# Linear attention and a token-mixing MLP on one core: nine casting DMAs of GpSimd issued in one row, and the second batch's k^T v in two halves

## The chip, the cores and the metric

The kernel runs on one core of a Trainium2 chip. The metric is the device time of one execution in microseconds (us). The engines are named as in the profile: PE (TensorE, matmuls; PEld its weight loads), DVE (VectorE), ACT (ScalarE), POOL (GpSimd) and SP (SyncE, which here only issues DMAs).

## The reference

```python
kv  = einsum('bhsd,bhse->bhde', k, v)          # k^T v per head
out = einsum('bhsd,bhde->bhse', q, kv)         # q.kv
out = out / sqrt(mean(out*out, -1) + 1e-6) * g_norm
x   = out with the heads side by side          # 8 batches, 576 tokens, 512 channels
u   = x + lam * (w_tok @ (alpha1 * x + beta1)) # mixing over tokens
y   = u + lam * (relu((alpha2 * u + beta2) @ w_ch1) @ w_ch2)
```

There are 8 batches, 8 heads, 576 tokens and a head size of 64; w_ch1 is 512 x 2048, w_ch2 2048 x 512. Inputs and output are float32.

## The kernel before, in words

**A planner orders everything.** `Prog.op` records each operation with its engine (or engines to choose from), a cost in us, what it reads and writes, and a priority. `schedule` plays the operations through a list scheduler: whenever an engine is free it takes the first ready operation of its queue in order of priority, and it also picks the PSUM banks. For DMAs it carries a model of the transfer: those of SP follow each other, those of POOL start some time after their issue (the line with `free[e] + 0.3`) and take their share from those of SP. The result is a fixed order for each engine, and `synchronize` adds the semaphore waits. An operation with `at=` has a fixed priority, and `after=` adds dependences that no data needs; `slack` lets the planner take an operation for ready that long after its inputs. A changed cost or gate can therefore move instructions on all engines; at run time each engine runs its list in order.

**The start.** The loads of q, k and v for the first batch come in two halves of the heads (L519, on SP). For each half PE makes k^T v (L616), transposes q (L584, L577) and makes q.kv (L706, L711). ACT squares (L743), DVE sums (L745), ACT and DVE make the reciprocal root (L748, L751), and DVE writes the normalized rows xm and their tail xtl (L767). Then `rt = xm * e_bc` (L771) and `xm = xm * g` (L774), here on POOL. `e_bc`, the product of alpha1, lam and g on all partitions, is made by PE (L1058) behind the second half's k^T v and copied by ACT (L506). Mixing over tokens is `tok_half`: L833 on PE with rt, then an addition by DVE (L845); PE transposes the result (L866), and the first layer of the MLP begins with L966 and goes on with L935. Until that first L966, PE fills its idle time with dummy matmuls on zeros (L1345) that the planner puts in.

**POOL's casting DMAs.** Weights in bfloat16 come by DMAs that cast, all issued by POOL: `w_tok` in four pieces and a rest (`wst`, L1112, and `wst4`, L1115), and `w_ch1` in four quarters (`w1`, L1267). Each has a priority and a gate in `after`, the load that must have landed before POOL may issue it:

```python
tgate = [("qf", 0), ("kf", 1)]                            # w_tok 0,1 / 2,3
gate = [("vf", 1), ("vf", 1), ("wst", 3), ("wst", 3)]     # w1 quarters 0 to 3
```

PE transposes w_tok with an identity matrix (L1159, L1180) and makes sums over its rows (L1202). The bias of the first layer, beta2 times w_ch1, is made by PE for each quarter (L1228) from b2hl, two small rows that POOL writes (L1071, L1073). SP loads the second batch's q, k and v only when the second quarter of w1 has landed. w_ch2 is loaded in float32 by SP (stg, L1274) and multiplied by lam on DVE or POOL (L1279).

**Further on.** The second batch's k^T v is one group of 144 small matmuls between groups of the first batch's first layer, its result copied by ACT and DVE in four copies (kvr, L506, L507). Then follow the second batch's q.kv, the second layer (L1000), mixing over tokens for the second batch (L799, L812), its transposes (L905), and the same stages for each later batch (first layer L950 for odd batches, L935 for even ones).

Of the kernel before, what the change touches and what calls it, by code (L numbers as in the profile page):

```python
# [54 lines left out]
class Prog:  # L55
# [79 lines left out]
    def schedule(self):  # L135
# [6 lines left out]
        free = {e: 0.0 for e in queues}  # L142
# [77 lines left out]
        while left:  # L220
            progressed = False
            for e, q in queues.items():
                while q and free[e] <= t + 1e-9:
# [64 lines left out]
                    if pick.lat is not None:  # L288
                        if e == "SP":
                            dma_free = max(dma_free, t + (2.5 if t < 3 else 1.25)) + pick.lat  # L290
                            pick.end = dma_free + 1.3
                            moving.append(pick)
                        elif e == "POOL":
                            s = max(free[e] + 0.3, pool_dma)
                            left_ = max(0.0, dma_free - s)
                            pool_dma = s + pick.lat + min(left_, pick.lat)
                            for y in moving:
                                if y.end - 1.3 > s:
                                    y.end += min(pick.lat, y.end - 1.3 - s)
                                    events.add(y.end)  # L300
                            dma_free = max(dma_free, s) + pick.lat
                            pick.end = pool_dma + 1.6
                        else:
                            pick.end = t + pick.lat + 3.0
                    else:
                        pick.end = free[e] + (0.35 if e == "PE" else 0.15)
# [110 lines left out]
def bass_transnormer_attn__then__resmlp_affine_kernel(  # L417
# [15 lines left out]
    with ExitStack() as stack:  # L433
        P = Prog(nc, stack)

        def sb(name, shape, dt):
            return stack.enter_context(nc.sbuf_tensor(name, shape, dt))
# [17 lines left out]
        kf = sb("kf", [128, 4, 9, DH], F32)  # L455
        vf = sb("vf", [128, 4, 9, DH], F32)
        qf = sb("qf", [128, 4, 9, DH], F32)
# [16 lines left out]
        wst4 = sb("wst4", [64, S], BF16)  # L474
        smask = sb("smask", [128, 128], BF16)
        w1 = sb("w1", [128, 4, FF], BF16)
# [7 lines left out]
        wst = ht[:].rearrange("p j t -> p (j t)")[:, 0:2304].rearrange("p (c s) -> p c s", c=4)  # L484
# [7 lines left out]
        def act_us(n):  # L492
            return 0.19 + n / 1200.0
# [15 lines left out]
        HALVES = (slice(0, 4), slice(4, 8))  # L509
# [4 lines left out]
        def halves(hs):  # L514
            return range(hs.start // 4, hs.stop // 4)
# [87 lines left out]
        def kv_groups(b, parts=ALL):  # L603
            def group(hs):
                t = P.ptile(2)
                h0, np_ = hs.start, (hs.stop - hs.start) // 4
                aa = halves(hs)

                def f(e):
                    for x_ in range(np_):  # L610
                        for c in range(9):
                            for i in range(2):
                                for y in range(2):
                                    x = h0 // 2 + 2 * x_ + i
                                    rows = slice(64 * y, 64 * y + 64)
                                    m = e.matmul(  # L616
                                        t.ap(slice(64 * i, 64 * i + 64))[
                                            :, y, 64 * x_:64 * x_ + 64],
                                        kf[rows, x, c], vf[rows, x, c], start=(c == 0),
                                        stop=(c == 8), tile_position=(64 * y, 64 * i))  # L620
                    return m
                P.op("PE", 0.2 + 1.06 * np_, f, cold=True, w=[t, ("kvp", hs.start)],
                     r=[("kf", a) for a in aa] + [("vf", a) for a in aa])

                def src(z):
                    return t.ap(slice(64 * z, 64 * z + 64))[:, :, 0:64 * np_].rearrange(
                        "p y (x d) -> p x y d", d=64)

                def heads(ap, z):
                    return ap[:, :, 2 * z:2 * z + 2]  # L630
                if b < R32:
                    prev = {}
                    for k_, (z, r_) in enumerate(((0, 0), (1, 0), (1, 1), (0, 1))):
                        o = heads(kvr[64 * r_:64 * r_ + 64, hs, 64 * r_:64 * r_ + 64].rearrange(
                            "p (x h) d -> p x h d", h=4), z)
                        prev[z] = [P.op(
                            "ACT" if k_ % 2 == 0 else "DVE",
                            act_us(128 * np_) if k_ % 2 == 0 else dve_us(128 * np_),
                            lambda e, o=o, z=z: copy(e, o, src(z)), hold=[t],
                            r=[("kvp", hs.start), "kvz"], w=[("kvr", a, z, r_) for a in aa],  # L640
                            after=prev.get(z, []))]
                    return
                kv5 = kvd[:].rearrange("p (x h) i d -> p x h i d", h=4)
                for z in range(2):
                    for r_ in range(2):
                        hi = heads(kv5[64 * r_:64 * r_ + 64], z)[:, :, :, 0]
                        P.op("ACT", act_us(256), lambda e, z=z, hi=hi: e.activation(  # L647
                            hi, src(z), ACT.Identity), r=[t], w=[("kvd", z, r_, 0)])
                for z in range(2):
                    for r_ in range(2):  # L650
                        hi, lo = (heads(kv5[64 * r_:64 * r_ + 64], z)[:, :, :, i]
                                  for i in range(2))
                        P.op("DVE", dve_us(256), lambda e, z=z, hi=hi, lo=lo: e.tensor_tensor(
                            out=lo, in0=src(z), in1=hi, op=ALU.subtract),
                            r=[t, ("kvd", z, r_, 0)], w=[("kvd", z, r_, 1)])
            for hs in parts:
                yield lambda hs=hs: group(hs)
# [447 lines left out]
        for i, hs in enumerate(HALVES):  # L1105
            for n in "kvq":
                load(n, 0, hs, sp["%s%d" % (n, i)])
        tgate = [("qf", 0), ("kf", 1)]
        wrows = moe_w_tok.rearrange("(u s c) t -> u s c t", s=32, c=9)
        for x in range(2):  # L1110
            for u in (2 * x, 2 * x + 1):
                P.op("POOL", 0.5, lambda e, u=u: e.dma_start(  # L1112
                    wst[:, u, :], wrows[u % 2, :, u // 2:u // 2 + 7:2]),
                    w=[("wst", u)], dma_us=0.85, at=-9003.0 + u, after=P.lastw[tgate[x]])
        P.op("POOL", 0.4, lambda e: e.dma_start(wst4[:], moe_w_tok[8:576:9, :]),  # L1115
             w=[("wst", 4)], dma_us=0.9, at=-8998.5, after=P.lastw[("wst", 3)])
        for n, dst, src in (("lam", lam_bc, moe_lam), ("a2", a2_bc[:], moe_alpha2),
                            ("g", g_bc[:], g_norm)):
            P.op("SP", 0.6, lambda e, dst=dst, src=src: e.dma_start(
# [1 line left out]
                 dma_us=0.8 if n != "g" else 0.3, at=sp[n])  # L1121
# [18 lines left out]
             w=["identb"])  # L1140
# [96 lines left out]
        def run(gens):  # L1237
            for gen in gens:
                for f in gen:
                    f()  # L1240
# [19 lines left out]
                    for i in range(2):  # L1260
                        P.readers.setdefault(("hth", j, i), []).append(o)

        gate = [("vf", 1), ("vf", 1), ("wst", 3), ("wst", 3)]

        def load_w(i):
            if i < 4:
                P.op("POOL", 0.9, lambda e: e.dma_start(  # L1267
                    w1[:, :, 512 * i:512 * i + 512], moe_w_ch1[
                        :, 512 * i:512 * i + 512].rearrange("(j p) f -> p j f", p=128)),
                    w=[("w1", i)], dma_us=2.6, at=-9000.0 + i, after=P.lastw[gate[i]])  # L1270
                bias_groups(i)
            else:
                n = i - 4
                P.op("SP", 0.6, lambda e: e.dma_start(  # L1274
                    stg[:, i % 3], moe_w_ch2[512 * n:512 * n + 512, :].rearrange(
                        "(j p) c -> p j c", p=128)), w=[("stg", i % 3)], dma_us=2.6,
                    at=sp["w%d" % i])
                for hh in range(4):
                    P.op(dve_pool(512), 0, lambda e, hh=hh: e.tensor_tensor(  # L1279
                        out=w2[:, 4 * n + hh, :], in0=stg[:, i % 3, hh], in1=lam_bc[:],  # L1280
                        op=ALU.mult), r=[("stg", i % 3), "lam"], w=[("w2p", n, hh)], pri=60,
                        after=u0, port=True)
                P.lastw[("w2", n)] = [y for hh in range(4) for y in P.lastw[("w2p", n, hh)]]
# [10 lines left out]
        load_kv(1, at=lambda n: sp["B" + n])  # L1294
        load_q(1, at=lambda n: sp["B" + n])
        u0 = P.lastw[("a2t", 0)] + P.lastw[("a2t", 2)]
        run([kv_groups(1), qt_groups(1)])
        for i in range(4, 8):
            load_w(i)
        for y in range(2):  # L1300
# [14 lines left out]
        for b in range(NB):  # L1315
# [17 lines left out]
            if more:  # L1333
                if b == 0:
                    P.op("POOL", 0.9, lambda e: e.memset(qtt[:], 0.0),
                         w=[("qt", 2, y) for y in range(2)])
# [45 lines left out]
```

## Time and profile before

| | |
|---|---|
| median of 9 runs | 366.28 us |
| lowest and highest run | 364.58 and 367.3 us |
| the profiled execution | 365.74 us, its span 363.7 us |
| PE busy | 351.6 us, 97% of the span |
| DVE, ACT, POOL busy | 211.0, 143.0, 115.8 us |
| DMA | 56.41 MB, mean 155 GB/s |
| granted clock, mean | 0.994 |

The span is the time from the first to the last instruction; the rest of the profiled execution's time lies around it. Busy PE is matmuls one after the other, also dummy ones. "Idle before" in a row is the idle time of the engine ahead of that instruction, with what ended it; "issue" means that the profile shows nothing that it waited for. The chain that ended last is followed back from the last instruction, at each step to what released it. The views of the chain, the timeline, the stretches and the DMA queues give times from the start of the span.

### The profile page before, as it was taken

The numbers are of one execution on the slowest core, as the hardware profiler recorded it, in microseconds if no ns is written. First come the engines' busy times: TensorE is split into PE (matmuls) and PEld (weight loads), VectorE is DVE, ScalarE is ACT, GpSimd is POOL, SyncE is SP. The second block draws the span as 40 slices with busy tenths as digits, with TensorE's granted clock in tenths as the row PEclk, the third lists the DMA queues.
The fourth block names the chain that finished last, engine by engine and source line by source line (L and its number), as shares of the span: only waits on it lengthen the run. The fifth ranks groups of instructions, "written<-read, shape, count | busy, mean of one in ns | idle before, by whom it ended". The sixth has DMA issues, their size and how long they took to land.

```text
span 363.7 us, 7875 instructions
## 1 busy us (share of the span) xinstructions
PE 351.6 (97%) x3504; PEld 210.8 (58%) x3296; DVE 211.0 (58%) x319; ACT 143.0 (39%) x253; POOL 115.8 (32%) x97
## 2 busy tenths in 40 slices
PE   8999799999999999999999999999999999999996
PEld 6977574366754554457654554457754554457644
DVE  3565779992577189733885189723884189620021
ACT  2763156327741156207730158007730156007600
POOL 3794177230065005800281015800661005400000
PEclk9999989999999999999999999999999999999999
DMA  7999994038775768557917694758945610331023
GB/s 285 214 213 349 383 383 183 0 45 110 206 285 111 120 162 329 101 111 128 370 32 113 123 309 154 102 113 140 357 62 106 140 31 0 74 87 31 0 59 87
DMA packets 67558, 56.41 MB, mean 155 GB/s; under 512 B 45552, under 2 KB 48452, under 8 KB 67524
## 3 DMA queue, kind: packets, MB, share of 16 engines
q1 hardware_dynamic: 64704, 53.14, 55.8%
q0 software_dynamic: 2768, 2.76, 4.8%
q8 instruction: 27, 0.44, 0.5%
q14 instruction: 7, 0.06, 0.0%
q10 hardware_dynamic: 52, 0.01, 0.0%
HBM read 38.60 MB, written 9.44 MB: 132 GB/s over the span
## 4 chain that ended last, share of the span: by engine, by line
PE 85%; DVE 6%; POOL 4%; issue 2%; DMA 2%; SPq 0%; ACT 0%; POOLq 0%; DVEq 0%
PE ps L1000 32%; PE ps L950 19%; PE ps L935 13%; PE ps L799 7%; PE ps L616 5%; PE ps L696 2%; PE ps L410 2%; DMA qf<-in_q_dram 2%; POOL rt L771 2%; POOL xm L774 1%; DVE rt L771 1%; PE ps L584 1%; PE ps L812 1%; DVE w L1279 1%; PE ps L966 1%
## 5 line engine op out<-in xcount | busy, mean ns | idle before, releaser
L1000 PE MATMUL ps<-w,ht 128*128 128x512 bf16 (+1 forms) x569 | 125.8, 373 | 1.8 <-issue 1.0
L1000 PEld LDWEIGHTS ps<-w,ht 128*128 128x128 bf16 x592 | 56.9, 98 | 64.0 <-issue 1.2
L924 ACT ACTIVATE ht<-ps,bias 128x640 bf16<-128x640 f32 (+2 forms) x100 | 73.5, 739 | 50.4 <-PE ps L950 37.9
L950 PE MATMUL ps<-a2t,w 128*128 128x320 bf16 x512 | 71.9, 299 | 0.0
L774 POOL TENSOR_TENSOR xm<-xm,g_bc 128x1024 f32<-128x1024 f32 (+1 forms) x18 | 36.2, 2012 | 109.7 <-DVE rt L771 109.2
L950 PEld LDWEIGHTS ps<-a2t,w 128*128 128x128 bf16 x512 | 49.4, 98 | 20.4 <-DVE xm L767 0.3
L935 PE MATMUL ps<-a2t,w 128*128 128x512 bf16 x231 | 54.0, 382 | 0.7 <-issue 0.2
L1011 DVE TENSOR_TENSOR xm<-ps,xm 128x512 f32<-128x512 f32 (+1 forms) x33 | 22.1, 672 | 52.4 <-PE ps L1000 52.4
L647 ACT ACTIVATE kvd<-ps 64x256 bf16<-64x256 f32 x24 | 9.1, 378 | 95.6 <-PE ps L616 95.4
L745 DVE TENSOR_REDUCE small<-sq 128x16 f32<-128x1024 f32 (+3 forms) x30 | 25.0, 846 | 23.0 <-ACT sq L743 22.8
L935 PEld LDWEIGHTS ps<-a2t,w 128*128 128x128 bf16 x240 | 22.7, 99 | 25.5 <-issue 0.6
L799 PE MATMUL ps<-rt,wt 128*128 128x512 bf16 x140 | 31.4, 379 | 0.4 <-DVE rt L771 0.4
L925 DVE TENSOR_SCALAR ht<-ps,bias 128x512 bf16<-128x512 f32 (+2 forms) x32 | 23.7, 745 | 11.7 <-PE ps L935 4.9
L548 POOL TENSOR_TENSOR qs<-qf,qs 128x512 bf16<-128x512 f32 x13 | 16.6, 1275 | 28.5 <-ACT qs L506 27.8
L743 ACT ACTIVATE sq<-ps 128x1024 f32<-128x1024 f32 (+3 forms) x30 | 21.7, 735 | 10.2 <-PE ps L410 8.2
L799 PEld LDWEIGHTS ps<-rt,wt 128*128 128x128 bf16 x140 | 13.6, 98 | 17.2 <-DVE rt L771 0.9
L783 DVE TENSOR_TENSOR xm<-ps,xm 128x512 f32<-128x512 f32 x28 | 19.0, 687 | 7.8 <-PE ps L799 7.5
L1011 DVE TENSOR_TENSOR xtl<-ps,xtl 128x512 f32<-128x512 f32 x4 | 2.8, 692 | 35.5 <-PE ps L1000 35.5
L785 POOL TENSOR_TENSOR a2b<-xm,a_bc 128x512 bf16<-128x512 f32 x12 | 17.4, 1450 | 14.9 <-DVE xm L783 9.5
L616 PE MATMUL ps<-vf,kf 64*64 64x64 f32 x1152 | 19.3, 220 | 3.0 <-issue 2.5
L616 PEld LDWEIGHTS ps<-vf,kf 64*64 64x64 f32 x1152 | 17.9, 135 | 6.1 <-issue 5.4
L767 DVE TENSOR_TENSOR xm<-ps,small 128x1024 f32<-128x1024 f32 (+1 forms) x20 | 20.1, 1004 | 0.3
(106 smaller groups left out, 331.6 us busy)
## 6 DMA issues: line engine op xcount, KB each, us to landing
kf<-in_k_dram SPq DMA_DIRECT2D x7, 1152.0 KB, 6.1
vf<-in_v_dram SPq DMA_DIRECT2D x7, 1152.0 KB, 9.8
qf<-in_q_dram SPq DMA_DIRECT2D x7, 1152.0 KB, 11.5
out_dram<-xm SPq DMA_DIRECT2D x62, 128.0 KB, 2.4
stg<-in_moe_w_ch_dram SPq DMA_DIRECT2D x4, 1024.0 KB, 16.6
w<-in_moe_w_ch_dram POOLq DMA_DIRECT2D x4, 512.0 KB, 8.6
kf<-in_k_dram SPq DMA_DIRECT2D x2, 576.0 KB, 6.0
vf<-in_v_dram SPq DMA_DIRECT2D x2, 576.0 KB, 7.1
```

What stands on the lines that cost most here:

```text
L616: m = e.matmul(t.ap(slice(64 * i, 64 * i + 64))[:, y, 64 * x_:64 * x_ + 64], kf[rows, x, c], vf[rows, x, c], start=(c == 0), stop=(c == 8) ...
L743: P.op("ACT", act_us(64 * m), lambda e: e.activation(both(sqv), raw(), ACT.Square), r=[t], w=[("sq", sqs)])
L745: P.op("DVE", dve_us(64 * m), lambda e: e.tensor_reduce(out=smv, in_=sqv, axis=AX.X, op=ALU.add), r=[("sq", sqs)], w=[("sm", sms)], pri=-20)
L767: P.op("DVE", dve_us(64 * m), lambda e: e.tensor_tensor(out=x3, in0=raw(), in1=inv(), op=ALU.mult), r=[t, ("sm", sms)], w=xk, pri=-200)
L774: P.op(dve_pool(64 * m) if b < 2 else "POOL", pool_us(64 * m), lambda e: e.tensor_tensor(out=x3, in0=x3, in1=gb, op=ALU.mult), r=xk + ["g" ...
L799: m = e.matmul(t.flat(), wt[:, sc if sc < 4 else 4 + b % 2, 128 * c:128 * c + 128], rt[:, rs(b, sc), :], start=(sc == 0), stop=(sc == 4))
L924: return e.activation(dst, src(), ACT.Relu, bias=bi)
L925: return e.tensor_scalar(out=dst, in0=src(), scalar1=bi, scalar2=0.0, op0=ALU.add, op1=ALU.max)
L935: m = e.matmul(t.flat(), w1[:, dj, 128 * fj:128 * fj + 128], a2t[:, dj, 0:512], start=(dj == 0), stop=(dj == 3))
L950: m = e.matmul(t.ap()[:, i, 0:320], w1[:, dj, 128 * fj:128 * fj + 128], a2t[:, dj, 320 * i:320 * i + 320], start=(dj == 0), stop=(dj == 3))
L1000: m = e.matmul(t.flat()[:, 0:m_], ht[:, fj, 128 * c:128 * c + 128], w2[:, fj, lo:hi], start=(fj == 0), stop=(fj == 15))
L1011: P.op("DVE", dve_us(m_), lambda e: e.tensor_tensor(out=x, in0=t.flat()[:, 0:m_], in1=x, op=ALU.add), r=[t] + keys, w=keys)
```

## The change

It does four things. All w_tok pieces and the first two quarters of w1 are now gated by the first half of q, and wst4 and the last two quarters by the second half of k; with the new priorities all nine casting DMAs stand in one row on POOL, ahead of the first product with e_bc. The planner's model has data of a POOL DMA start 1.2 instead of 0.3 us after the issue, the issue costs 0.6 or 0.8 us, and the loads of w1 get a slack of 1.0. And the second batch's k^T v is recorded in two halves of the heads (36 matmuls of the code each, every one of which shows as two in the profile).

```diff
-                            s = max(free[e] + 0.3, pool_dma)
+                            s = max(free[e] + 1.2, pool_dma)
...
-        tgate = [("qf", 0), ("kf", 1)]
+        tgate = [("qf", 0), ("qf", 0)]
...
-                P.op("POOL", 0.5, lambda e, u=u: e.dma_start(
+                P.op("POOL", 0.6, lambda e, u=u: e.dma_start(
                     wst[:, u, :], wrows[u % 2, :, u // 2:u // 2 + 7:2]),
                     w=[("wst", u)], dma_us=0.85, at=-9003.0 + u, after=P.lastw[tgate[x]])
-        P.op("POOL", 0.4, lambda e: e.dma_start(wst4[:], moe_w_tok[8:576:9, :]),
-             w=[("wst", 4)], dma_us=0.9, at=-8998.5, after=P.lastw[("wst", 3)])
+        P.op("POOL", 0.6, lambda e: e.dma_start(wst4[:], moe_w_tok[8:576:9, :]),
+             w=[("wst", 4)], dma_us=0.9, at=-8998.0, after=P.lastw[("kf", 1)])
...
-        gate = [("vf", 1), ("vf", 1), ("wst", 3), ("wst", 3)]
+        gate = [("qf", 0), ("qf", 0), ("kf", 1), ("kf", 1)]
...
-                P.op("POOL", 0.9, lambda e: e.dma_start(
+                P.op("POOL", 0.8, lambda e: e.dma_start(
                     w1[:, :, 512 * i:512 * i + 512], moe_w_ch1[
                         :, 512 * i:512 * i + 512].rearrange("(j p) f -> p j f", p=128)),
-                    w=[("w1", i)], dma_us=2.6, at=-9000.0 + i, after=P.lastw[gate[i]])
+                    w=[("w1", i)], dma_us=2.6, at=-8999.5 + i, after=P.lastw[gate[i]],
+                    slack=1.0)
...
-        run([kv_groups(1), qt_groups(1)])
+        run([kv_groups(1, HALVES), qt_groups(1)])
```

The built order of POOL in the changed kernel: four w_tok pieces, quarters 0 and 1, wst4, quarters 2 and 3, the cast of b2hl, two products rt, xm, rt's tail, xm, b2hl's difference, xtl, and then the second half (two rt, its tail, two xm). On PE the transposes of wst4 and their sums stand ahead of L966, and four L935 stand between the halves of the second batch's k^T v.

## The prediction

> **What bounds the kernel now.** I began with the page's second part, the 40 slices, each 9.1 us long.
>
> ```profile
> PE   8999799999999999999999999999999999999996
> ...
> PEclk9999989999999999999999999999999999999999
> DMA  7999994038775768557917694758945610331023
> ```
>
> TensorE (PE) is busy everywhere; the only dent after the first slice is the fifth, 36 to 45 us, and the only dip of its clock is in the slice behind it. DMA is full up to 55 us. So a change to the start pays only by what it takes off PE before about 75 us; from there the rows are PE without holes. Next I read the chain that ended last, in order of time, for the start.
>
> ```profile
> 15.43 1.28 POOL rt L771
> ...
> 18.06 0.29 issue
> 18.35 0.59 POOL wst L1115
> 18.94 0.31 POOL w L1267
> 19.25 0.45 issue
> 19.70 0.76 POOL w L1267
> 20.46 0.77 POOL rt L771
> ...
> 28.82 1.28 POOL xm L774
> ...
> 31.81 3.49 PE ps L966 x32
> ```
>
> From 15.43 to 30.10 GpSimd (POOL) is the chain. Ahead of that it waits 1.37 us for e_bc (its timeline says); it multiplies, and at 18.06 stops multiplying for 2.40 us to issue three casting DMAs. 1.71 us after its last product, at 31.81, PE starts the first layer of the MLP. The third view is PE's timeline, the fourth the busy time in stretches of 3.41 us (columns: PE, weight loads, DVE, ACT, POOL, granted clock, DMA share, GB/s).
>
> ```profile
> 39.44 2.17 PE L616 MATMUL ps<-vf,kf 64*64 64x64 f32 x124
> 44.15 0.47 PE L616 MATMUL ps<-vf,kf 64*64 64x64 f32 x17 [2.54 <-issue]
> ```
>
> ```profile
> 42.17:45.58 3.41, 1.27 (x25) 0.91 (x26) 2.64 (x4) 0.76 (x3) 0.65 (x1) 1.00 1.01 375
> 45.58:48.99 3.41, 3.41 (x15) 2.53 (x14) 1.35 (x3) 1.66 (x3) 2.19 (x2) 0.50 1.02 374
> 48.99:52.40 3.41, 3.41 (x26) 2.76 (x24) 3.02 (x5) 2.00 (x4) 2.14 (x3) 1.00 1.05 390
> ```
>
> In the middle of the second batch's k^T v PE stops for 2.54 us and waits for nothing but "issue". The DMA view of 40 to 46 us has the reason: beside the data there is one packet on the instruction queue.
>
> ```profile
> q1 hardware_dynamic: 1101, 2.24, 101.2%
> q8 instruction: 1, 0.02, 1.1%
> ```
>
> The page's 27 such packets carry 0.44 MB, 16 KB each. k^T v is PE's densest stretch of instructions (288 weight loads and matmuls in 2.3 us); I read the hole as PE out of instructions while the next block stands behind data. After the hole PE runs 3.41 us at half clock.
>
> **The change part by part.** Durations are of the profiled execution, 365.74 us (span 363.7, 2.04 around it); the median of the nine runs is 0.54 higher, and the sum is put on the median.
>
> *A. POOL's issues.* Out of the chain: 18.06 to 20.46, 2.40 us. Into the wait: the built order now has nine DMAs in one row behind the bias products, gated on q (first half) and k (second half), which landed at 8.57 and 10.07 (landings are the last semaphore of a DMA in the trace). From 9.38, where the first issue stood: 4 x 0.604 (w_tok) + 4 x 0.776 (w1) + 0.592 (wst4) = 6.11, so 15.49; then the small cast of b2hl, 0.21: 15.70. ACT wrote e_bc by 15.35, so POOL's own issues end last, and rt begins 0.27 later than before. Inside the chain the new order puts b2hl's difference (0.20 + 0.07) and the first half's tail product (0.72 + 0.08) ahead of the second half: +1.07. Net -2.40 + 0.27 + 1.07 = -1.06. The second half's normalized rows, which DVE finished at 21.1 and 22.1, are asked for by POOL at about 23.0 and 24.3, so 1.9 us of delay there is covered. Ends: -2.40 (what is inserted hides) and 0, or worse if issuing itself slows (first rival). SP waits for the second w1 quarter (landed 22.78) before it loads the second batch; nothing is put ahead of that quarter, so SP's queue moves with POOL's or stays.
>
> The casting DMAs now compete with the last v and q loads, which landed at 11.57 and 13.66. The casts ran at about 200 GB/s when alone (DMA view, 16 to 26 us); two w_tok pieces of 144 KB ahead of q cost at most 1.4 us, less than the cover above: I take 0, with ends 0 and +0.9 (both v and q late by as much, 2.8). [...]
>
> *B. PE's order.* The transposes of wst4 (chain: 39.13 to 39.59, 0.46) and their row sums (five L1202, 0.42) move ahead of L966, where PE waits for POOL and fills with dummy matmuls; one more group of bias matmuls (L1228 x16, 0.38) moves behind it. Net -0.50. If that cover were gone, +0.88 comes back: end +0.38.
>
> *C. The hole.* Counting weight loads and matmuls in the built order, PE ran dry at number 1198. In the changed order number 1198 is 86 instructions into the second half of k^T v, since four L935 now stand between the halves. From the first L966 to dry: before 41.61 - 31.81 = 9.80; after 9.80 - 0.46 + 0.38 + 0.87 (four L935) - 0.20 (24 instructions fewer of k^T v) = 10.39. If the block is asked for at the same place of the stream and takes as long, PE resumes 44.15 - 31.81 = 12.34 after the first L966: hole 1.95, -0.59. Ends: it vanishes (-2.54), or the block comes at the same absolute time and the hole is 3.0 (+0.5). I take the value between, since the DMA is as full either way.
>
> *D. The half clock.* From the chain, L584 x8, L577 x2 and L935 x4 took 1.71 + 0.43 + 1.27 in it and 0.87 + 0.22 + 0.88 just after: 1.44 us. The stretch before it held 1.98 us of idle PE. A hole of 1.95 lies wholly in one 3.41 us stretch in (3.41 - 1.95) / 3.41 = 43% of phases; so 57% of 1.44: -0.82, ends 0 and -1.44. The row shows that a window with 1.27 us of work is enough for the half clock, and I go by it. The Trainium skill ("TensorE: Matmul & The Clock Gate", Part 1) has the clock halve after a free-running window of about 3.4 us that is idle. By its words a part-idle window would not do it and the whole 1.44 would go.
>
> *E. DVE from 51 to 74 us.* The chain runs on DVE there and PE waits 0.41 (L799) and 0.22 (L905). DVE gets seven products of w2 instead of nine (2 x 0.69 less; POOL, idle then, takes them at 1.27) and four copies of 0.28 instead of two of 0.44; and PE has twelve more L1000 (2.6 us) ahead of L799. I take -0.30, ends -0.63 and +0.6. The second batch's q landed at 43.98 and its first transpose would now stand at about 44.5: hidden, by half a microsecond.
>
> Sum: -1.06 - 0.50 - 0.59 - 0.82 - 0.30 = -3.27; 365.74 becomes 362.5, the median 363.0.
>
> **The rivals.**
> 1. *The software queue backs up* (ends slower). Before, six casting DMAs were issued by 14.06 and the other three only at 18.35; now nine go out by 15.5, with the first not landed before 14.29. Every issue row took 0.55 to 0.78 with up to six under way, which speaks against it; nine were never under way. If the last two w1 issues had to wait for the first w1 quarter (landed 20.15), POOL would start multiplying at 20.15 + 1.55 + 0.21 = 21.9 instead of 15.4: 6.5 - 2.40 + 1.07 = 5.2 later, less B to E (2.2): 3.0 slower, 369.3. It decides from 3.3 us of blocking on.
> 2. *The block of instructions comes at its absolute time.* Then PE resumes at 44.15 whatever A and B gain, having done four L935 (0.87) and the L1202 (0.42) already, less 0.20: -1.09, with E -1.4, the clock as before: 364.9. For it: the DMA is full without a break from 28 to 58 us, and a later request would stand in the same line. Against: the line itself should move with the second w1 quarter.
> 3. *The start doesn't move*: the casts make v and q late over their cover, POOL waits for DVE at 23, and A is 0 to +0.9 instead of -1.06. With B to E (-2.2): 364.1 to 365.0.
>
> **How the numbers follow.** Forecast case 0.58 (361 to 365), rival 2 0.20, rival 1 0.12, rival 3 0.10. This measurement can tell about 0.3%, 1.1 us: faster means below 365.2. Faster: 0.52 of the 0.58, 0.13 of rival 2, 0.05 of rival 3, together 0.70. Slower: rival 1 and 0.05 from the bad ends of C to E in the others, 0.17. The rest, 0.13, the same. The low end takes a hole that vanishes (1.95 more) and gives back a tenth of that: 361.2; the high end takes in rivals 2 and 3 and leaves out rival 1: 366.8.
>
> **What would show it.** Right: nine POOL issues in a row from 9.4 to 15.5, the first rt product at 15.7, the end of the last xm product near 29.0, the first L966 near 30.7, the hole in the second half of k^T v near 2 us, the clock row at 1.00 or one stretch at 0.50. Wrong: POOL issue rows of over 1 us (rival 1); PE resuming at 44 (rival 2); PE idle before the second L616 at 11.5 or POOL waiting for DVE near 23 (rival 3); or a new issue hole in a later k^T v.

## The result, and the profile after

The changed kernel took 364.52 us in the median of 16 runs (363.37 to 365.84), the kernel before, run beside it, 366.81 us in the median of 53. The ratio is 0.9937, interval 0.9921 to 0.9952: 2.3 us faster. The forecast was 363.0 (3.3 us faster), range 361.2 to 366.8. The profiled execution took 363.37 us, span 361.2, against 365.74 and 363.7.

The page's slices of the kernel after:

```profile
PE   8999698999999999999999999999999999999996
...
PEclk9999999999999999999999999999999999999999
```

The dent of the fifth slice is still there, and deeper. The dip of the clock behind it is gone. POOL's timeline after (start, length, what, number, idle before):

```profile
9.12 2.37 POOL L1112 DMA_DIRECT2D ht<-in_moe_w_tok_dram  x4 [0.64 <-POOL w L1081]
11.42 1.56 POOL L1267 DMA_DIRECT2D w<-in_moe_w_ch_dram  x2
12.90 0.61 POOL L1115 DMA_DIRECT2D wst<-in_moe_w_tok_dram  x1
13.44 1.60 POOL L1267 DMA_DIRECT2D w<-in_moe_w_ch_dram  x2
...
15.32 2.63 POOL L771 TENSOR_TENSOR rt<-xm,e_bc 128x512 bf16<-128x512 f32 x2
...
26.34 2.68 POOL L774 TENSOR_TENSOR xm<-xm,g_bc 128x512 f32<-128x512 f32 x2
```

Nine issues stand in one row and end at 15.04; none takes over 0.86 us. The last product ends at 29.02 (before 30.10). PE's timelines show what came of it, first the line of L966 before, then the rows after:

```profile
31.65 3.66 PE L966 MATMUL ps<-a2t,w 128*128 128x256 bf16 x32
```

```profile
30.86 3.66 PE L966 MATMUL ps<-a2t,w 128*128 128x256 bf16 x32
...
38.68 1.28 PE L616 MATMUL ps<-vf,kf 64*64 64x64 f32 x72
40.12 0.81 PE L935 MATMUL ps<-a2t,w 128*128 128x512 bf16 x3 [0.16 <-issue]
40.86 0.92 PE L616 MATMUL ps<-vf,kf 64*64 64x64 f32 x44
44.44 0.68 PE L616 MATMUL ps<-vf,kf 64*64 64x64 f32 x28 [2.66 <-issue]
```

The first L966 comes 0.79 us earlier (30.86 for 31.65). The hole, now in the second half of k^T v, is no shorter: PE runs dry at 41.77 and resumes at 44.44, against 44.15 before. The stretches around the hole:

```profile
39.62:43.03 3.41, 2.00 (x71) 1.29 (x65) 2.66 (x3) 0.96 (x2) 2.59 (x2) 1.00 1.05 388
43.03:46.45 3.42, 1.85 (x36) 1.51 (x37) 1.19 (x4) 0.82 (x3) 1.21 (x2) 1.00 0.95 347
46.45:49.86 3.41, 3.41 (x26) 2.58 (x25) 2.78 (x5) 1.95 (x4) 3.25 (x3) 1.00 1.05 389
```

The hole is split between two stretches and neither is followed by 0.50; that is the larger part of the gain in this pair of profiles (the prediction put a stretch at half clock at 1.44 us). What comes behind is in the chain that ended last:

```profile
49.65 4.27 DVE w L1280 x3
...
55.88 0.67 DVE xm L767
56.59 1.04 PE ps L935 x4
```

DVE's three w2 products (L1280 is L1279 of before) take 1.42 us each on average, between 0.98 and 1.76, while POOL works through seven of its own (46.01 to 56.8), and PE waits 0.99 us, until 56.59, for the normalized rows.

The two profiles differ by 2.23 us where the third batch's first layer begins, here before and after:

```profile
82.61 9.94 PE L950 MATMUL ps<-a2t,w 128*128 128x320 bf16 x72
```

```profile
80.38 8.86 PE L950 MATMUL ps<-a2t,w 128*128 128x320 bf16 x64
```

From there to the end of the span they are within 0.3 us. By stage: to the first L966 -0.79; from there to PE's resumption +1.08 (13.58 for 12.50, but with four L935 and the L1202 already done, worth 1.29); from the end of the hole to L950 -2.52 (35.94 for 38.46).

### The profile page after: what moved, and what is told of

Read it like the earlier page. It is cut to its first block, busy times and chain, and to the rows that moved or that the text cites. A ratio compares the mean times of both kernels' runs of the same rounds, so it can differ in the third digit from the quotient of the medians.

```text
span 361.2 us, 7878 instructions
## 1 busy us (share of the span) xinstructions
PE 350.1 (97%) x3506; PEld 210.6 (58%) x3299; DVE 209.8 (58%) x321; ACT 144.7 (40%) x258; POOL 115.4 (32%) x94
## 4 chain that ended last, share of the span: by engine, by line
PE 92%; DMA 2%; DVE 2%; issue 2%; SPq 1%
PE ps L1000 34%; PE ps L950 19%; PE ps L935 13%; PE ps L799 8%; PE ps L616 5%; DMA vf<-in_v_dram 2%; PE ps L696 2%; PE ps L410 2%; DVE w L1280 1%; PE ps L812 1%; PE ps L833 1%; PE ps L966 1%; PE ps L584 1%; PE ps L1159 1%; PE ps L1346 1%
## 5 line engine op out<-in xcount | busy, mean ns | idle before, releaser
L924 ACT ACTIVATE ht<-ps,bias 128x640 bf16<-128x640 f32 (+2 forms) x102 | 75.3, 741 | 48.8 <-PE ps L950 37.1
L950 PE MATMUL ps<-a2t,w 128*128 128x320 bf16 x512 | 71.5, 299 | 0.0
L774 POOL TENSOR_TENSOR xm<-xm,g_bc 128x1024 f32<-128x1024 f32 (+1 forms) x16 | 33.4, 2090 | 108.8 <-DVE rt L771 108.2
L950 PEld LDWEIGHTS ps<-a2t,w 128*128 128x128 bf16 x512 | 49.5, 98 | 20.1
L935 PE MATMUL ps<-a2t,w 128*128 128x512 bf16 x230 | 53.4, 379 | 1.8 <-DVE xm L767 1.0
L935 PEld LDWEIGHTS ps<-a2t,w 128*128 128x128 bf16 x240 | 22.4, 98 | 26.1 <-DVE xm L767 1.5
L799 PE MATMUL ps<-rt,wt 128*128 128x512 bf16 x140 | 31.4, 379 | 0.0
L925 DVE TENSOR_SCALAR ht<-ps,bias 128x512 bf16<-128x512 f32 (+2 forms) x30 | 21.8, 732 | 11.8 <-PE ps L935 5.3
L799 PEld LDWEIGHTS ps<-rt,wt 128*128 128x128 bf16 x140 | 13.7, 98 | 16.5
```

The source lines that it names most:

```text
L774: P.op(dve_pool(64 * m) if b < 2 else "POOL", pool_us(64 * m), lambda e: e.tensor_tensor(out=x3, in0=x3, in1=gb, op=ALU.mult), r=xk + ["g" ...
L799: m = e.matmul(t.flat(), wt[:, sc if sc < 4 else 4 + b % 2, 128 * c:128 * c + 128], rt[:, rs(b, sc), :], start=(sc == 0), stop=(sc == 4))
L924: return e.activation(dst, src(), ACT.Relu, bias=bi)
L925: return e.tensor_scalar(out=dst, in0=src(), scalar1=bi, scalar2=0.0, op0=ALU.add, op1=ALU.max)
L935: m = e.matmul(t.flat(), w1[:, dj, 128 * fj:128 * fj + 128], a2t[:, dj, 0:512], start=(dj == 0), stop=(dj == 3))
L950: m = e.matmul(t.ap()[:, i, 0:320], w1[:, dj, 128 * fj:128 * fj + 128], a2t[:, dj, 320 * i:320 * i + 320], start=(dj == 0), stop=(dj == 3))
```

## The experiments

Each ratio is to runs of the kernel before on the same chip in the same sitting; their medians were 367.62, 366.99 and 367.11 us. "Clock lost" of a run is its span times one minus the granted clock that the run recorded. A stretch of 3.41 us at 0.50 shows as 1.7, and it costs time only as far as PE works in it; the time before the clock first opens is not in it.

**The two parts alone.** The kernel before with the halves only, and the change without them:

```diff
-        run([kv_groups(1), qt_groups(1)])
+        run([kv_groups(1, HALVES), qt_groups(1)])
```

> The kernel before with the second batch's k^T v in two halves and nothing else of the change. Its built order is that of before up to the first half of k^T v (instruction 944 of PE, weight loads and matmuls counted); between the halves stand only the five L1202, so PE runs dry (number 1198) 100 instructions into the second half, some 0.3 us later than before. Theory (the block of instructions comes at its own time, 44.1 to 44.4 us, whatever PE has done by then): hole 2.2 to 2.5 us, PE resumes at 44.2; about the time of before, -0.4 to +0.3 us, with the half clock as often as in before. Rival (the halves are what pays in the change, since they take the half clock away): 1 to 1.5 us faster than before.

> The whole change but for the halves: k^T v of the second batch stays one group. The built order is that of the changed kernel up to k^T v, so first L966 at 31.0 and k^T v from 38.7. Theory (block at its own time): PE dry at 40.7, resumes at 44.2 to 44.5, a hole of 3.5 us, longer than any so far, and the half clock behind it; the 0.8 us gained at L966 are lost in the hole: 365 to 366.8, that is 0.5 to 2.2 us slower than the changed kernel. Rival (the block comes a fixed time after its place in the stream, 12.3 us after the first L966): resumes at 43.4, hole 2.6, and most of the gain of the change is there without the halves: 364.3 to 365.

Halves alone: ratio 1.0027 (1.0006 to 1.0049), a loss. Issues alone: 0.9981 (0.9955 to 1.0008), a gain that can't be told from none. Together they gave 0.9937, so the parts don't add up. Of the two theories put down for the halves alone, neither fits: PE did not resume at 44.2 but at 45.93, and there was no gain. The first line is PE's timeline of the halves alone, the second that of the issues alone:

```profile
45.93 0.57 PE L616 MATMUL ps<-vf,kf 64*64 64x64 f32 x22 [2.81 <-issue]
```

```profile
44.34 0.58 PE L616 MATMUL ps<-vf,kf 64*64 64x64 f32 x24 [3.29 <-issue]
```

With the issues alone PE comes to the hole earlier (dry at 41.05) and waits longer, as its theory expected; but no half clock followed in this execution, which took 364.48 us, 2.45 less than the median of its runs. The halves alone shorten nothing for certain: 2.81 us, in an execution whose first L966 began 1.0 us later than in the first profile.

**The hole taken away, first padding.** 64 tiny matmuls of two columns in sixteen of the first thirty dummies move PE's stream by 128 instructions, in the kernel before and in the changed one:

```diff
+        count = [0]
...
+            count[0] += 1
+            if 6 < count[0] <= 22:
+                for _ in range(4):
+                    e.matmul(t.flat()[:, 0:2], wz[:, 0:128], wz[:, 0:2], start=True, stop=True)
+                return e.matmul(t.flat()[:, 0:64], wz[:, 0:128], wz[:, 0:64], start=True, stop=True)
```

> The kernel before, with 64 tiny matmuls (2 columns; 128 instructions with their weight loads) among the dummy matmuls ahead of the first k^T v, sixteen of which are made narrower to make room; nothing else moves. It shifts the borders of PE's 16 KB blocks by half a block against the work. Theory (the hole is PE out of instructions): the block that is late is asked for 128 instructions earlier, near 29 us, and PE passes the second batch's k^T v without a hole; the next limit is the second batch's q (landed at 43.98), so the first transpose of it stands near 44.0 instead of 46.0, and the half clock is gone where it was: 2 to 3.5 us faster than before, 363.3 to 364.8. Rival (the hole is something else, data or PSUM): nothing changes, within 0.5 us of before.

> The changed kernel with the same 64 tiny matmuls. Theory (out of instructions): the hole of 2.66 us in the second half of k^T v goes, q of the second batch (43.3) is just in time, the clock stays whole: 2 to 2.7 us faster than the changed kernel, near 362. What the change is worth without the hole on either side (its start, PE's order) is then this run against the padded kernel before: theory 1.0 to 1.5 us. Rival (the hole is something else): no difference from the changed kernel.

The hole is gone from the second batch's k^T v in both. Ratios 0.9927 (0.9890 to 0.9963) and 0.9925 (0.9898 to 0.9952): on the kernel before, the padding is worth as much as the change; on the changed kernel it brings nothing more (363.93 and 364.50 us), where the expectation had about 362 and 1.0 to 1.5 us between the two. The padding has a price at the start: the clock opens at 9.16 and 10.49 us (4.62 and 5.49 without it), and the first L966 stands at 32.38 and 32.25 (31.65 and 30.86 without it). The waits of PE of the padded changed kernel (total, times, longest) say what stands in the place of the hole:

```profile
PE ps L799 <- DVE rt L771: 1.6, 1, 1.6
PE ps L616 <- issue: 1.1, 1, 1.1
...
PE ps L935 <- DVE xm L767: 0.7, 1, 0.7
```

In the padded kernel before, the longest waits there are 0.8 us for a first-layer result (L925) and 0.6 us (L845). The changed order runs into DVE, and into a new hole in the next k^T v at 79 us.

**A cheaper padding that wasn't one.** The 128 or 256 instructions added by replacing later dummies (128 x 256) with tiny matmuls (the code is that of the first two runs; the third has 96 for 64, and 32 more among dummies 21 to 28):

```diff
+        count, left = [0], [64]
...
+            count[0] += 1
+            if count[0] > 30 and left[0] > 0:
+                left[0] -= 4
+                for _ in range(4):
+                    e.matmul(t.flat()[:, 0:2], wz[:, 0:128], wz[:, 0:2], start=True, stop=True)
+                return e.matmul(t.flat()[:, 0:2], wz[:, 0:128], wz[:, 0:2], start=True, stop=True)
```

> The kernel before with the 64 tiny matmuls (128 instructions) in the dummy matmuls that come after the first thirty, each of sixteen dummies being replaced by five tiny ones, so that PE's warming up at the start is as in before (in the first padded pair the clock opened only at 9 to 10 us and the first L966 stood 0.6 to 1.2 later). Theory (out of instructions): no hole in the second batch's k^T v, L966 where before has it or up to 0.5 us later, 2.5 to 4 us faster than before by the ratio, lost clock 0 to one stretch. Rival (the first padded kernel gained by something else, such as its cold start): the gain of 2.7 us shrinks below 1.5.

> The changed kernel with the same shift of half a block in the later dummies. Theory: no hole, first L966 at 31.0 to 31.5, faster than the changed kernel by 1 to 2.5 us (ratio to before near 0.990), DVE then ends the wait of L799. What the change is worth without the hole is this against the padded before: theory 0 to 1 us, since the half clock and the hole go in both. Rival (the start is what pays): 1 us or more between the two padded kernels.

> The changed kernel shifted by a whole block: 128 tiny matmuls, 256 instructions, 32 of them in the first thirty dummies and 96 in the later ones. Theory (16 KB blocks of 256 instructions): borders stand where they stood, so the hole is back in the second half of the second batch's k^T v, 2 to 3 us, at 43 to 45 us. Rival (any extra instructions ahead remove it, by time or by depth of the queue): no hole.

A miss, and a lesson of its own. Ratios 0.9966 (0.9939 to 0.9992) and 1.0007 (0.9979 to 1.0035); the third, 366.64 us in its one run. The hole was gone in all three, in the third too, against the expectation; but its start was 6 us later than the changed kernel's, so it doesn't control for anything. In it the packet on the instruction queue stands at 45.31, 0.2 us behind the first matmul of k^T v; in the seven profiles with the hole it stands 2.4 to 3.9 us behind. So the block came in time there, and the run decides nothing about where blocks end. The clock rows of the page, in the order of the three runs, and two stretches of the third:

```profile
PEclk9789999999999999999999999999999999999999
```

```profile
PEclk9858999999999999999999999999999999999999
```

```profile
PEclk9759999999999999999999999999999999999999
```

```profile
10.02:13.43 3.41, 2.92 (x98) 2.75 (x99) 1.28 (x2) 2.24 (x6) 3.41 (x7) 1.00 1.12 251
13.43:16.85 3.42, 3.42 (x42) 3.08 (x30) 2.17 (x6) 1.33 (x4) 2.24 (x4) 0.50 0.76 99
```

There are two to four stretches at half clock at 13 to 29 us, in the part of the start whose dummies had been replaced. The first row has PE busy for 2.92 us of 3.41, 30 of its 98 matmuls having two columns, and the clock is halved behind it all the same. (The padded kernel before gained less than the first time, and the padded changed kernel nothing: 365.57 and 367.19 us.)

**The row g.** The changed kernel with g's row read as 128 different rows of q:

```diff
-                dst, src[None, :].to_broadcast([128, src.shape[0]])), w=[n],
+                dst, src[None, :].to_broadcast([128, src.shape[0]]) if src is not g_norm
+                else q[0, 0, 0:128, :]), w=[n],
```

> The changed kernel with g_bc loaded from 128 different rows of q instead of one row of g_norm repeated on 128 partitions: the same 32 KB in the same 256-byte pieces, the same order on every engine, other values (the output is not the reference's: g is left out). In the changed kernel the casts' bandwidth falls from 160 to 31 KB per us at 15 us while pieces of g_bc trickle in from 14 to 18 us, and the second w1 quarter lands at 23.5, later than before (22.8) although issued 1.1 us earlier. Theory A (reading one row 128 times holds all DMA engines up): the dip goes, g_bc lands by 14, the second w1 quarter lands by 22.3, SP loads the second batch about 1.2 us earlier, and the hole shrinks by as much. Theory B (small pieces are slow, or the casts' own making of descriptors leaves the dip): nothing moves by over 0.5 us.

g's transfer landed at 16.6 instead of 18.1, but the second w1 quarter only at 23.0 instead of 23.5 and the second batch's q at 42.6 instead of 43.3. The hole was 2.94 us, the time 365.43, in one run. Neither theory fits whole: g came 1.5 us sooner, but the rest of the line only 0.5 to 0.7. The slow trickle of g's small pieces is not what keeps the rest of the DMA line in place.

**The early wait for w1.** In the profile of the halves alone PE waited 1.0 us at 20.3 us for the first w1 quarter, and a stretch at half clock followed. So I moved that one product in the kernel before, and nothing else, and took a second profile of the kernel before, unchanged:

```diff
-    __slots__ = ("eng", "cost", "fn", "deps", "alloc", "tiles", "pri", "idx",
+    __slots__ = ("late", "eng", "cost", "fn", "deps", "alloc", "tiles", "pri", "idx",
...
-        self.sequence = sorted(self.ops, key=lambda o: (o.start, o.idx))
+        self.sequence = sorted(self.ops, key=lambda o: (getattr(o, "late", None) or o.start, o.idx))
...
-            P.op("PE", 0.6, f, r=[("w1", i), "b2", "b2h"], w=[t, ("bp", i)], pri=-30)
+            P.op("PE", 0.6, f, r=[("w1", i), "b2", "b2h"], w=[t, ("bp", i)], pri=-30).late = 23.41 if i == 0 else None
```

> The kernel before with one thing moved: the bias product of the first w1 quarter (L1228 x16) goes behind the first fourteen L833 instead of ahead of the row sums L1202, about 2.3 us later in PE's stream; every other instruction keeps its place. Theory E (early stretch): in the kernel before, PE reaches that product at 20.6 us, half a microsecond after the first w1 quarter landed (20.15 in the profile); where the quarter lands a little later PE stops for about a microsecond and a half-clock stretch of 3.41 us follows, worth 1.8 us. By it the median of the clock lost falls from 3.65 to about 1.8 us and the time by 1 to 2.5 us (ratio 0.993 to 0.997), while the hole in the second batch's k^T v stays at 2.5 to 3.3 us, since no instruction ahead of it is added or taken away. Theory L (only the late stretch varies): the clock is lost behind the hole alone; nothing changes, ratio 0.999 to 1.001, clock lost 3.65.

> The kernel before unchanged, for a second profile of it. Its runs lose 3.65 us to the clock in the median, two stretches, while the profile at hand shows one (45.58 to 48.99). Theory E: the other stretch lies at 20 to 27 us, behind a wait of L1228 for the first w1 quarter. Theory L: both lie next to each other at 42 to 50 us. If this execution has only one stretch, it lies behind the hole and nothing is decided.

Theory E falls: ratio 0.9998 (0.9975 to 1.0020), clock lost 2.0 us in the median against 2.2 of the kernel before in that sitting. The second profile of the kernel before (368.37 us) has its lost clock all in one place. Its timeline of PE, and its stretches:

```profile
32.57 3.66 PE L966 MATMUL ps<-a2t,w 128*128 128x256 bf16 x32
...
40.37 2.16 PE L616 MATMUL ps<-vf,kf 64*64 64x64 f32 x124
46.52 0.71 PE L616 MATMUL ps<-vf,kf 64*64 64x64 f32 x17 [3.99 <-issue]
```

```profile
41.08:44.50 3.42, 1.45 (x98) 1.31 (x90) 2.97 (x3) 0.00 (x0) 1.77 (x1) 1.00 1.06 391
44.50:47.91 3.41, 1.20 (x22) 0.99 (x23) 0.58 (x2) 0.52 (x2) 0.23 (x1) 0.50 1.04 383
47.91:51.33 3.42, 3.27 (x13) 2.45 (x13) 0.96 (x2) 1.39 (x5) 3.17 (x3) 0.50 1.05 386
```

The same program, and a hole of 3.99 us where the first profile had 2.54. It covers about 2 us of each of two stretches, and both are followed by 0.50 (the second and the third row). In the run with the moved product the hole was 3.73 us, again with two stretches. So the profile that the prediction rested on was a favourable execution of the kernel before: of its 68 runs in the three sittings, 46 lost more than 3 us of clock, two stretches or more.

The place of the hole, other than its length, is the same everywhere. Counted in the traces, PE ran dry after 1196 to 1199 weight loads and matmuls in all seven profiles that have the hole, of six kernels, whose first L966 stands anywhere from 30.86 to 32.67 us.

**A clean padding.** The tiny matmuls go among the last eight of the first thirty dummies, when the clock is already open, and fifteen dummies there are cut to 64 columns; the dummies of the later start stay whole:

```diff
+        count = [0]
...
-            return e.matmul(t.flat()[:, 0:256], wz[:, 0:128], wz[:], start=True, stop=True)
+            count[0] += 1
+            if 22 < count[0] <= 30:
+                for _ in range(8):
+                    e.matmul(t.flat()[:, 0:2], wz[:, 0:128], wz[:, 0:2], start=True, stop=True)
+            n = 64 if 22 < count[0] <= 37 else 256
+            return e.matmul(t.flat()[:, 0:n], wz[:, 0:128], wz[:, 0:n], start=True, stop=True)
```

> The kernel before with 64 tiny matmuls (2 columns) added among the last eight of the first thirty dummies, after the clock has opened, and the dummies 23 to 37 cut from 256 to 64 columns to pay for them: 128 instructions more ahead of everything, dummies of the later start untouched. By the theory that the hole is a block boundary falling into dense k^T v, the hole of 2.5 us there goes, and with it the half-clock stretch behind it; the early stretch may stay. Price of the padding 0 to 0.5 us, first L966 at 31.7 to 32.2. Time 362.5 to 364.5, ratio 0.988 to 0.994. By the theory that dummies near the start set the clock, cutting 23 to 37 costs stretches again: 365 to 368.

> The changed kernel with the same padding as the run above. If the change's worth lies in the issues, in the order of PE and in the clock of the early start, it keeps 0.8 to 2 us against the padded kernel before: 361.0 to 363.0, ratio 0.984 to 0.990. If its whole worth was that the hole and the clock fell differently, the two padded kernels are the same within 0.3%: 362.5 to 364.5. No hole in the second batch's k^T v; the wait for DVE's w2 products (L935 or L799) stays at 0.7 to 1.6 us; a later issue wait of about 1 us may appear, as with the first padding.

On the kernel before 0.9920 (0.9898 to 0.9941), 363.85 us; on the changed one 0.9945 (0.9927 to 0.9964), 364.72 us. PE's timeline of the first, at the place of the hole:

```profile
40.29 2.40 PE L616 MATMUL ps<-vf,kf 64*64 64x64 f32 x141
...
43.20 0.81 PE L935 MATMUL ps<-a2t,w 128*128 128x512 bf16 x3 [0.16 <-issue]
44.99 1.09 PE L584 MATMUL ps<-ident,qf 128*128 128x128 f32 x8 [0.98 <-DMA qf<-in_q_dram]
```

No hole, and PE is so early that it waits 0.98 us for the second batch's q: the cover of half a microsecond that the prediction saw for that transfer is used up. The time is as the theory of the block boundary had it; the first L966 (32.49) is 0.3 us later than expected. In the padded changed kernel PE runs dry in other k^T v instead:

```profile
13.37 0.91 PE L616 MATMUL ps<-vf,kf 64*64 64x64 f32 x43 [0.98 <-issue]
...
80.54 0.81 PE L616 MATMUL ps<-vf,kf 64*64 64x64 f32 x38 [1.32 <-issue]
```

These holes begin after 443 and 1953 weight loads and matmuls, that of the unpadded changed kernel after 1197: 754 and 756 apart, three times about 252. This fits holes that stand at the borders of blocks, with some 252 of them to a block (an estimate from these three counts). Behind the first of these holes, at 12.4 us, a stretch at half clock follows (16.27 to 19.68), and L966 begins only at 34.04. That padding was thus no clean control for the changed kernel, while the first one (its start 1.4 us later than the unpadded changed kernel's, but with no early hole) was fairer. Both pairs agree in one thing: with the hole of the second batch taken away, the change is worth nothing that these runs can measure. But neither pair keeps the earlier start that the change has without padding (L966 0.79 us earlier; 0.13 earlier in the first pair, 1.55 later in this one), and the padded changed kernel has holes and waits of its own. What the start is worth by itself is thus not separated. No version beat both kernels beyond doubt: the best, the padded kernels before at 0.9920 and 0.9927, lie inside or next to the interval of the change, 0.9921 to 0.9952.

## Why the prediction was right, and where it was off

The forecast (faster, 363.0) was right in its sign, and its size was 1 us too large. Term by term:

- **A, POOL's issues: -1.06 predicted.** POOL gained 1.08, and the rows came as listed (issues to 15.04, first rt at 15.32, last product at 29.02), helped by a first issue at 9.12 instead of 9.38, behind a load that the change doesn't touch. Only 0.79 reached the first L966: PE is the chain itself from 11.27 on in the profile after, and its own order sets L966. The term named POOL's gain and took it for PE's.
- **The casts' competition: 0.** PE waited only 0.18 us there, for v at 11.27. The transfers didn't come sooner either: the second w1 quarter, issued 1.1 us earlier, landed at 23.5 instead of 22.78, and SP's load of the second batch began 0.7 later with it. The Trainium skill ("DMA: Bandwidth & Descriptors", Issuing engines are not separate DMA queues) says that the DMAs of all issuing engines run on the same 16 engines and interleave. The trace agrees: between 9 and 16 us the queue of POOL's casts has 59.0% and that of SP's loads 40.1% of the 16 engines' time.
- **B, PE's order: -0.50.** The moves took place. The five L1202 and the transposes stand ahead of L966, and 32 instead of 16 L1228 behind L935. Being part of what now limits PE before L966, they took something off A's gain; the two weren't separated.
- **C, the hole: -0.59.** Failed in the profile: 2.66 instead of 1.95. The place was right: PE ran dry 88 instructions into the second half, predicted 86, though 10.74 us behind the first L966 (by the chain, 41.77 - 31.03) instead of 10.39. The step that failed is "the block takes as long". PE resumed at 44.44, as the second rival had it (44.15). The reason isn't the rival's absolute time, however: the same kernel before resumed at 44.15 in one execution and at 46.52 in another. In the records of the instruction queue the block's packet stands at 41.72 and 44.16 in these two, 2.4 and 3.9 us behind the first matmul of k^T v, and PE resumes 2.43 and 2.36 us behind the packet. After: packet at 42.02, resumption 2.42 later. What varies is the time at which the packet is served, in a DMA that is full (101.2% in the view of the prediction). What the packet stands behind, the runs don't show.
- **D, the half clock: -0.82.** Undersized. In the profiles the whole 1.44 went. In the runs more did: the kernel before loses 3.66, 3.65 and 2.19 us of clock in the median of its three sittings (25, 23 and 20 runs), the changed kernel 0.73, with nine of the seventeen runs whose clock is on record at or under 0.73 and the others at one stretch. The prediction took one stretch at 57% from one favourable profile, while most runs of the kernel before have two; that its hole is often nearer 4 us is seen in two profiles only (3.99, and 3.73 with the moved product). The clock isn't all of it. Where less than 1 us was lost, the two kernels are close: 364.4 us in the mean of five runs before, 364.1 in nine after (from different sittings). Where one stretch was lost they are 1.9 apart, 366.8 in seventeen runs and 365.0 in eight; how long the hole was in these runs is not on record. The rule of the Trainium skill ("TensorE: Matmul & The Clock Gate", Part 1) that the clock halves after an idle window is too narrow here: windows with 1.27, 1.45 and 1.20 us of busy PE were followed by 0.50.
- **E, DVE: -0.30.** Wrong sign: the old waits at L799 (0.41) and L905 (0.22) went, and a new one of 0.99 came at L935: +0.36. The step that failed is the duration of L1280: 0.69 each was taken, and 1.42 was measured for three of them while POOL worked through seven of its own. The profile before could have said so: there too the DVE products that began while one of POOL's was under way took longer (1.75 at 41.61, 1.20 at 48.68, 1.46 at 52.23), and those that began with POOL idle 0.68 or 0.69.

By the two profiles the sum comes out as -0.79 (A), -0.50 (B), +0.12 (C), -1.44 (D) and +0.36 (E), -2.25, where the first L950 moved by -2.23; B is the predicted value here, as it wasn't measured by itself. So the forecast held because D gave more and A, C and E less than was said; that these errors nearly cancel is luck.

Rival 1 is dead: nine software DMAs went out at 0.56 to 0.86 us each. Rival 3 is wrong: the start moved. Rival 2 described the profile after best in when PE resumes; but it had the clock as before, and a fixed time is out: PE resumed at 45.93 with the halves alone and at 46.52 in the second profile of the kernel before.

The padded kernels before show that the hole and the clock behind it are worth as much as the whole change (0.9927 and 0.9920). That the change gains by the same means is read from the profiles, where the clock is 1.44 of 2.23 us, and from the clock of the runs; the 0.79 us of the start stand beside it in the profiles, and no run separates the two. Why the halves lose alone and pay with the issues is only argued: they put 1 us of L935 between the request for the block and the place where it is missed, and the phase of the hole against the stretches of the clock decides the rest. That phase was not set by any run.

## What to carry to other kernels

A hole with "issue" in a dense row of small matmuls may have its place from the count of instructions, and not from the work around it (here behind 1196 to 1199 of them, in six kernels), and its length from when the next block comes. So count instructions, and try a padding before rebuilding a schedule; 128 instructions were enough here. When one profile shows a stall, take a second profile of the same program before pricing it; here the same hole was 2.54 and 3.99 us, and the stretches of half clock behind it were one and two. And where an engine off the chain gets shorter, price the chain that takes over, here PE's own order and DVE beside a busy POOL.

## What the runs showed of the hardware

- The stretches at half clock lie on a grid of 3.41 us, counted from where the clock first opens: at 4.62 us in the one profile of the kernel before (half clock from 45.58, twelve steps on), at 6.96 in the other (from 44.50, eleven steps on). The hole cost no stretch (where it was 2.66 and 3.29 us long), one (2.54, 2.81, 2.94) or two (3.73, 3.99); so its length alone doesn't say, and how it lies on the grid counts too.
- PE's busy time doesn't say whether the clock will be halved: a row with 2.92 us busy of 3.41 was followed by 0.50 (30 of its 98 matmuls had two columns), and in the first run of the cheap padding even one that was busy throughout (9.88 to 13.29, 45 of its 104 the same), while rows with 1.85 and 2.00 us around the hole of the changed kernel, and with 1.57 and 1.81 around that of the issues alone, were not. What the gate does count was not settled.
- Where sixteen dummies of 256 columns had been made tiny, two and four stretches at half clock stood in the first 30 us (one profile of each kernel).
- In seven profiles with the hole (2.54 to 3.99 us long) PE resumed 2.4 to 2.7 us behind the packet on the instruction queue, whatever its length.
